# One state block per corner of the array, and triangular output products cut into 64x64 tiles, in a fused RWKV and feed-forward kernel

## The chip, the cores and the metric

The kernel runs on one NeuronCore of a Trainium2 chip. The metric is the device time of one execution in microseconds (us). Times below are the median of three runs, and one further execution was profiled. TensorE is called PE in the profile (PEld is its loading of weights), VectorE DVE, ScalarE ACT, GpSimd POOL, SyncE SP.

## The reference

A linear attention with a decaying state runs over 768 steps for 4 batches of 8 heads of width 48, and its output goes through a feed-forward layer with 384 inputs and 2048 hidden columns. Cut to what matters:

```
for t in range(S):
    y[:, :, t] = r_t @ (state + (u * k_t) v_t^T)
    state = w_t[:, None] * state + k_t v_t^T
x = y.transpose(0, 2, 1, 3).reshape(B * S, H * D)      # 3072 x 384
h = x @ w_in
out = (h * sigmoid(1.702 * h)) @ w_out
```

## The kernel before

**Chunks.** Tokens go in 24 chunks of 128 (t = 0 to 23), six per batch, so that chunks 0, 6, 12 and 18 start without a state and chunks 5, 11, 17 and 23 leave none. Heads go in four pairs p; the even head of a pair lies on partitions 0 to 63 (16 of them zeros) and the odd one on 64 to 111. `chunk(t)` is a generator of twelve steps: two scans of the decays (L252, L258), the scaled k and r in `kq` (L273, L274), the diagonal `s`, the decay of the old state (L292), the transposes of k (ps_t), `update` (products ps_u at L332 and the new state), `diagonal` (eight ACT copies into `am`, L321), the scores (L359) copied into `am` under the mask `after` (L362), the output products, and `split` (L222 on ACT, L223 on DVE), which leaves the output as a high and a low part in the tile x. `fill_x` (L425, POOL) moves parts of x for the feed-forward layer when a group of four chunks is complete.

**Two layouts.** For chunks 0 to 11 the state `sf` of a pair is a block of 112 rows by 96 columns, in which the rows of one head meet zeros in the columns of the other. The output goes to one tile, ps_y: L399 multiplies `am` (128 tokens by 128 tokens, zero below the diagonal) by v, with the two heads in two column halves of the array (128x64 tiles), and L407 adds the state's part, also with 128x64 tiles. For chunks from 12 on (`cross`) the state is `sx`, 48 columns per pair without zeros, two of the four pairs have their heads swapped, and the output goes to two tiles ps_c: L371 does the state's part in 64x64 tiles (four at once), L377 the part of `am` in 128x64 tiles over all 128 columns.

**Feed-forward.** 96 tasks (six groups i of four chunks, 16 slices f of hidden columns each). A task multiplies x by a slice of w_in into a tile ph (two buffers), `gelu` makes gh, gf (ACT) and gl (DVE), and two tasks later the second product adds into three tiles po. Tasks 32 to 94 run as `rows_of`: their products are cut into two row halves of the array (64x128 tiles) that run beside each other. When the last second product of a group is done, `store` copies its three po tiles to ob on ACT (L587), and the next group's second products write the same three tiles.

**Order.** Everything is in the order written: first the string RAMP (tasks before 32 and the chunks 0 to 12, part of 13), then `rest`, which gives each chunk's steps a place relative to the tasks. An output and its `split` stand right before the `update` and `diagonal` of the next chunk. Each engine works through its own queue in that order. At two places, after chunk 16 and after chunk 20, a group ends there: ACT's queue has the split, the eight `diagonal` copies, then the three ob copies, then the next gelu.

Of the kernel before, what the change touches and what calls it, by code (L numbers as in the profile page):

```python
# [21 lines left out]
P = 128  # L22
NP = H // 2
R = 2 * D
HB = 64
# [59 lines left out]
def rwkv_ffn_kernel(ctx: ExitStack, tc, wkr, vp, vrk, ub, w_in, w_out, masks, vt, uc, out):  # L85
# [26 lines left out]
    after = cp.tile([P, C], F32, name="after")  # L112
# [5 lines left out]
    after_b = after.bitcast(I32).unsqueeze(1).broadcast_to([P, NP, C])  # L118
    u_heads = hm[:, 2:].rearrange("r (p h) -> r p h", h=2)
# [10 lines left out]
    states = [at.tile([R2, TOP + NP * R], F32, tag=f"sf{i}", name="sf") for i in range(2)]  # L130
    crossed = [at.tile([R2, TOP + NP * D], F32, tag=f"sx{i}", name="sx") for i in range(2)]
# [7 lines left out]
    def behind_moves(dma):  # L139

        if len(moves) == 2 * NM:
            tc.add_manual_dep(dma.ins, moves[-1], SYNC, reason="the first group's x is wanted sooner")
        return dma

    def load(t):
# [7 lines left out]
        if t < CROSS:  # L153
            for c0, c1 in ((0, n), (n, a.shape[1])) if t < 2 else ((0, a.shape[1]),):
                if c0:
                    yield
                behind_moves(queue[0].dma_start(a[first:last, c0:c1], rows[:, c0:c1]))
        else:
            for c0, w in ((1, CW), (n, C), (n + NP * C, C)):
                for odd in range(2):  # L160
                    cols = slice(c0 + odd * 2 * w, c0 + (odd + 1) * 2 * w)
                    for half in range(2):
                        dst, src = TOP + half * D, (half ^ odd) * D
                        queue[0].dma_start(a[dst : dst + D, cols], wkr[t, src : src + D, cols])  # L164
        yield
        assert t < 3 or t - 3 in weighed
        queue[0].dma_start(v[:, TOP:], vrk[t, :, 0:DM])
        if t >= WHOLE:
            rk = pools["late"].tile([P, 2 * DM], F32, tag="rk", name="rk_t")
            queue[0].dma_start(rk, vrk[t, :, DM:])  # L170
# [68 lines left out]
    def chunk(t):  # L239
# [7 lines left out]
        first, final = t % CB == 0, (t + 1) % CB == 0  # L247

# [24 lines left out]
        V.tensor_tensor(kf, k, li[:, :, 1:CW], op=ALU.mult)  # L273
# [37 lines left out]
        cross = t >= CROSS  # L311
        name = lambda p, r_: 2 * p + (r_ ^ p // 2 if cross else r_)

        def diagonal():

            for h in range(2):
                x_ = at.tile([P, NP, C], F32, tag=f"am{h}", name="am")
                am.append(x_)
                for p in range(NP):
                    j = name(p, h)  # L320
                    A.activation(x_[:, p], ident, AF.Copy, scale=s[:, j : j + 1])  # L321

        def update():
# [9 lines left out]
            if cross:  # L333
                new = state[t] = crossed[t % 2]
                flat = ps_u.rearrange("r p d -> r (p d)")
                if sf is None:
                    A.copy(new[:, TOP:], flat)
                else:
                    V.tensor_tensor(new[:, TOP:], flat, sf[:, TOP:], op=ALU.add)
                return  # L340
            new = state[t] = states[t % 2]
            news, olds = (y[:, TOP:].rearrange("r (p h d) -> r p h d", p=NP, h=2) for y in (new, states[1 - t % 2]))
            for h in range(2):
                if sf is None:
                    A.copy(news[head(h), :, h], ps_u[head(h)])
                else:
                    V.tensor_tensor(news[head(h), :, h], ps_u[head(h)], olds[head(h), :, h], op=ALU.add)
# [13 lines left out]
        for h in range(2):  # L361
            V.copy_predicated(am[h], after_b, ps[h])  # L362
        yield
        cs = slice(col * C, (col + 1) * C)
        if cross:
            ps = [ps_a.tile([R2, 2, C], F32, tag="psa", name=f"ps_c{r_}") for r_ in range(2)]
            each = [(p, r_, r_ ^ p // 2) for p in (0, 2, 1, 3) for r_ in range(2)]
            if sf is not None:
                for p, r_, o in each:
                    c = p * D  # L370
                    T.matmul(  # L371
                        ps[r_][head(o), p % 2], sf[head(r_), c + o * TOP : c + HB], qf[head(r_), p],
                        start=p in (0, 2), stop=False, skip_group_check=True,
                    )
            for p, r_, o in each:
                c = (2 * p + o) * D
                T.matmul(  # L377
                    ps[r_][head(o), p % 2], v[:, c + o * TOP : c + HB], am[r_][:, p],
                    start=sf is None and p in (0, 2), stop=p in (1, 3), skip_group_check=True,
                )  # L380
# [39 lines left out]
    def fill_x(x, c0, c1, cross=False):  # L420

        for m in range(NM):
            for i, dst in enumerate((R2, 0)):
                j = TOP * (2 * m + i + 1)
                move = G.dma_start(  # L425
                    x[dst : dst + TOP, :, m ^ 2 * (cross and i == 0), c0:c1].bitcast(F32),
                    x[j : j + TOP, :, NM ^ 2 * (cross and j >= HB), c0:c1].bitcast(F32),
# [17 lines left out]
    def first_product(j, task):  # L445
# [5 lines left out]
        x = xs.get((i, 0), xs[i])  # L451
# [69 lines left out]
    def first_rows(j, half):  # L521
# [5 lines left out]
        for n in range(3 * NM):  # L527
# [5 lines left out]
                half, ("h", j), parts[j], w, xs[i][:, x, c ^ 2 * (half and starts[i] >= CROSS), cs],  # L533
# [47 lines left out]
    def store(i, start, N, order=range(NM)):  # L581
# [12 lines left out]
        xs.pop((i, 0), None)  # L594
# [5 lines left out]
    with tc.manual_schedule():  # L600
# [17 lines left out]
        def do(token):  # L618
# [7 lines left out]
            elif kind == "x":  # L626
                group, col = where[i]
                if col == CHUNKS[group] - 1:
                    fill_x(xs[group], 0, (col + 1) * C, i >= CROSS)
            elif kind == "c":  # L630
                x = xs[i, 0] = new_x(i)
                for c in range(NM):
                    for rows, src in ((slice(0, HB), c), (slice(HB, P), c ^ 2)):
# [188 lines left out]
```

## Time and profile before

| what | value |
|---|---|
| median of three runs | 507.99 us (507.67 to 508.84) |
| the profiled execution | 508.05 us |
| its span, first to last instruction | 506.1 us |
| PE, busy | 494.2 us, 98% |
| DVE, busy | 290.6 us, 57% |
| ACT, busy | 283.9 us, 56% |
| granted TensorE clock, mean | 0.997 of full speed |

The span and the profiled execution's time differ by 1.95 us, which lie before the first and behind the last instruction. Busy time is the union of an engine's instructions. The duration of one matmul contains its way through the array, so that matmuls overlap; how fast they follow one another is read from the distance of their starts.

### The profile page before, as it was taken

The numbers are of one execution on the slowest core, as the hardware profiler recorded it, in microseconds if no ns is written. First come the engines' busy times: TensorE is split into PE (matmuls) and PEld (weight loads), VectorE is DVE, ScalarE is ACT, GpSimd is POOL, SyncE is SP. The second block draws the span as 40 slices with busy tenths as digits, with TensorE's granted clock in tenths as the row PEclk, the third lists the DMA queues.
The fourth block names the chain that finished last, engine by engine and source line by source line (L and its number), as shares of the span: only waits on it lengthen the run. The fifth ranks groups of instructions, "written<-read, shape, count | busy, mean of one in ns | idle before, by whom it ended". The sixth has DMA issues, their size and how long they took to land.

```text
span 506.1 us, 11444 instructions
## 1 busy us (share of the span) xinstructions
PE 494.2 (98%) x4535; PEld 416.5 (82%) x4535; DVE 290.6 (57%) x451; ACT 283.9 (56%) x618; POOL 95.5 (19%) x200
## 2 busy tenths in 40 slices
PE   7999999999999999999999999999999999999994
PEld 3766777888888888888888888888888888888873
DVE  7899999999987213656456555555555322111210
ACT  4987889978865533465455465554564533323222
POOL 2002000000100200076304376303460002210000
PEclk9999999999999999999999999999999999999998
DMA  8996960125465300045112245111350001140001
GB/s 269 308 378 188 332 218 7 58 93 189 127 181 126 84 1 1 0 132 138 32 49 48 79 115 153 42 40 33 96 156 2 1 1 33 69 121 1 1 1 69
DMA packets 19471, 50.30 MB, mean 99 GB/s; under 512 B 4545, under 2 KB 8321, under 8 KB 19409
## 3 DMA queue, kind: packets, MB, share of 16 engines
q1 hardware_dynamic: 11664, 31.24, 19.3%
q0 software_dynamic: 7344, 17.72, 13.7%
q8 instruction: 38, 0.62, 0.5%
q10 hardware_dynamic: 400, 0.53, 0.3%
q14 instruction: 25, 0.20, 0.1%
HBM read 40.82 MB, written 4.72 MB: 90 GB/s over the span
## 4 chain that ended last, share of the span: by engine, by line
PE 82%; DVE 5%; ACT 4%; DMA 2%; issue 1%; POOL 1%; SPq 0%; ACTq 0%; DVEq 0%
PE po L512 26%; PE ph L512 24%; PE ps_s L359 3%; PE po L486 3%; PE ph L454 3%; PE po L487 3%; PE po L488 3%; PE ph L455 3%; PE ph L456 3%; PE ps_c L377 2%; DMA raw<-in_w_in 2%; PE ps_y L399 1%; PE ps_u L332 1%; PE ps_c L371 1%; PE ps_y L407 1%
## 5 line engine op out<-in xcount | busy, mean ns | idle before, releaser
L512 PE MATMUL ph<-x,pair 64*128 64x512 f32 x1134 | 185.5, 376 | 0.0
L472 DVE TENSOR_TENSOR gl<-gf,gh 128x512 fp32r<-128x512 f32 x96 | 66.3, 690 | 183.5 <-ACT gf L471 182.7
L512 PE MATMUL po<-gh,pair 64*128 64x512 f32 x768 | 157.6, 384 | 0.2 <-SPq L517 0.2
L512 PEld LDWEIGHTS ph<-x,pair 64*128 64x128 f32 x1134 | 143.5, 186 | 14.1
L471 ACT ACTIVATE gh<-ph 128x512 fp32r<-128x512 f32 x84 | 50.1, 597 | 157.7 <-PE ph L512 137.0
L512 PEld LDWEIGHTS po<-gh,pair 64*128 64x128 f32 x768 | 95.7, 186 | 10.4 <-issue 1.1
L512 PE MATMUL po<-gl,pair 64*128 64x512 f32 x384 | 99.2, 376 | 0.0
L425 POOL DMA_DIRECT2D x<-x x36 | 18.2, 512 | 248.5 <-DVE x L223 207.4
L321 ACT ACTIVATE am<-ident,s 128x128 f32<-128x128 f32 x192 | 58.8, 396 | 2.5 <-issue 1.5
L164 POOL DMA_DIRECT2D wkr_t<-in_wkr x108 | 53.8, 505 | 10.9 <-DVE kq L273 6.2
L512 PEld LDWEIGHTS po<-gl,pair 64*128 64x128 f32 x384 | 50.0, 186 | 4.8
L471 ACT ACTIVATE gf<-ph 128x512 f32<-128x512 f32 x84 | 49.8, 593 | 0.0
L454 PE MATMUL ph<-x,pair 128*128 128x512 f32 x99 | 39.0, 394 | 0.4 <-ACT gf L467 0.4
L456 PE MATMUL ph<-x,pair 128*128 128x512 f32 x99 | 38.0, 384 | 0.2 <-DVE pair L213 0.2
L455 PE MATMUL ph<-x,pair 128*128 128x512 f32 x99 | 37.9, 383 | 0.0
L486 PE MATMUL po<-gh,pair 128*128 128x512 f32 x96 | 37.8, 394 | 0.0
L488 PE MATMUL po<-gl,pair 128*128 128x512 f32 x96 | 36.9, 385 | 0.0
L487 PE MATMUL po<-gh,pair 128*128 128x512 f32 x96 | 36.8, 383 | 0.0
L228 ACT ACTIVATE junk<-lp 112x1032 bf16<-112x1032 f32 x24 | 25.6, 1068 | 12.3 <-DVE lp L258 12.2
L252 DVE TENSOR_TENSOR_SCAN lp<-wkr_t,d1r 112x516 f32<-112x516 f32 x24 | 29.4, 1225 | 1.3 <-DMA wkr_t<-in_wkr 1.0
L258 DVE TENSOR_TENSOR_SCAN lp<-wkr_t,d1f 112x516 f32<-112x516 f32 x24 | 29.4, 1225 | 0.1
L362 DVE COPY_PREDICATED am<-after,ps_s 128x512 f32<-128x512 int32 x40 | 26.9, 727 | 1.4 <-PE ps_s L359 1.2
(92 smaller groups left out, 645.0 us busy)
## 6 DMA issues: line engine op xcount, KB each, us to landing
wkr_t<-in_wkr SPq DMA_DIRECT2D x10, 770.5 KB, 5.3
raw<-in_w_out SPq DMA_DIRECT2D x6, 1024.0 KB, 11.4
raw<-in_w_in SPq DMA_DIRECT2D x5, 1024.0 KB, 10.9
wkr_t<-in_wkr POOLq DMA_DIRECT2D x72, 48.0 KB, 2.1
rk_t<-in_vrk POOLq DMA_DIRECT2D x9, 384.0 KB, 3.5
out_t<-ob POOLq DMA_DIRECT2D x12, 256.0 KB, 2.7
v_t<-in_vrk SPq DMA_DIRECT2D x15, 192.0 KB, 4.6
rk_t<-in_vrk SPq DMA_DIRECT2D x7, 384.0 KB, 3.4
```

The costliest lines, as they stand in the source:

```text
L164: queue[0].dma_start(a[dst : dst + D, cols], wkr[t, src : src + D, cols])
L252: V.tensor_tensor_scan(li.rearrange("r p c -> r (p c)")[:, ::-1], w1[:, ::-1], d1r.rearrange("r p c -> r (p c)")[:, ::-1], 0.0, op0=ALU.mu ...
L321: A.activation(x_[:, p], ident, AF.Copy, scale=s[:, j : j + 1])
L454: T.matmul(o, h_, halves(x[:, 0, c, cs], plain), start=c == 0, stop=False)
L455: T.matmul(o, h_, halves(x[:, 1, c, cs], plain), start=False, stop=False)
L456: T.matmul(o, l_, halves(x[:, 0, c, cs], plain), start=False, stop=c == NM - 1)
L471: A.activation(g, ph, AF.Gelu_apprx_sigmoid, scale=1.0 / W_SCALE)
L472: V.tensor_tensor(gl, gf, gh.bitcast(F32), op=ALU.subtract)
L486: T.matmul(o, h_, halves(gh, plain), start=first, stop=False, skip_group_check=True)
L487: T.matmul(o, l_, halves(gh, plain), start=False, stop=False, skip_group_check=True)
L488: T.matmul(o, h_, halves(gl, plain), start=False, stop=f == NF - 1, skip_group_check=True)
L512: mm = T.matmul(by_twos(out), w[rows], halves(x[rows]), start=start, stop=stop, skip_group_check=True)
```

## The change

Chunks 0 to 11 take the state without zero blocks too: `sf` has 48 columns per pair, the decay handles 192 columns instead of 384, the new state is one operation instead of two, and the state's product for the even head uses rows and columns 0 to 63, for the odd head rows and columns 64 to 111 (two opposite corners of the array, both into ps_y).

For chunks from 12 on, the products of `am` and v are cut in two halves of 64 source tokens. The half-matrix of `am` that is zero for the earlier 64 target tokens is left out: per pair and head there is one 64x64 tile over 128 columns and one over 64. The two halves go to two tiles ps_c, which hold partial sums; a tile `yt` collects them (two ACT copies, four DVE additions), and then `split` works on all of yt. In the two swapped pairs the order of source tokens is turned by halves, so that both row halves of the array get the same work: the loads of v, r, k bring swapped halves, `kf` is written turned, and a turned identity and a turned mask are made once in the step `u`. The layout of x is the same for all groups, so the step `c` (six POOL moves) goes.

```
-    states = [at.tile([R2, TOP + NP * R], ...) for i in range(2)]
-    crossed = [at.tile([R2, TOP + NP * D], ...) for i in range(2)]
+    states = [at.tile([R2, TOP + NP * D], ...) for i in range(2)]
...
+        if cross:
+            pairs_ = slice(0, NP // 2)
+            V.tensor_tensor(kf[:, pairs_], k[:, pairs_], li[:, pairs_, 1:CW], op=ALU.mult)
+            V.tensor_tensor(out_[:, :, ::-1], *ins_, op=ALU.mult)
+        else:
+            V.tensor_tensor(kf, k, li[:, :, 1:CW], op=ALU.mult)
...
-            for h in range(2):
-                if sf is None:
-                    A.copy(news[head(h), :, h], ps_u[head(h)])
-                else:
-                    V.tensor_tensor(news[head(h), :, h], ps_u[head(h)], olds[head(h), :, h], op=ALU.add)
+            if sf is None:
+                A.copy(new[:, TOP:], flat)
+            else:
+                V.tensor_tensor(new[:, TOP:], flat, sf[:, TOP:], op=ALU.add)
...
         if cross:
-            ps = [ps_a.tile([R2, 2, C], F32, tag="psa", name=f"ps_c{r_}") for r_ in range(2)]
+            ps = [ps_a.tile([R2, NP, C], F32, tag="psa", name=f"ps_c{r_}") for r_ in range(2)]
...
-            for p, r_, o in each:
-                c = (2 * p + o) * D
-                T.matmul(
-                    ps[r_][head(o), p % 2], v[:, c + o * TOP : c + HB], am[r_][:, p], ...
+            for p, halves_ in ((0, (0, 1)), (2, (1, 0)), (1, (0, 1)), (3, (1, 0))):
+                for i_ in halves_:
+                    for r_ in range(2):
+                        o = r_ ^ p // 2
+                        c, rows, c0 = (2 * p + o) * D, slice(i_ * HB, (i_ + 1) * HB), HB * (i_ ^ p // 2)
+                        T.matmul(
+                            ps[i_][head(o), p, c0:], v[rows, c + o * TOP : c + HB], am[r_][rows, p, c0:], ...
...
-            for b, y in enumerate(ps):
-                split(*(xs[i][0:R2, n_, 2 * b : 2 * b + 2, cs] for n_ in range(2)), y)
+            yt = at.tile([R2, NP, C], F32, tag="rku", name="yt")
+            for b, y in enumerate(ps):
+                two = slice(2 * b, 2 * b + 2)
+                A.copy(yt[:, two], y[:, two])
+            for b, y in enumerate(ps):
+                two = slice(2 - 2 * b, 4 - 2 * b)
+                for rows, cols in ((slice(0, HB), slice(HB, C)), (slice(HB, R2), slice(HB if sf is None else 0, C))):
+                    V.tensor_tensor(yt[rows, two, cols], yt[rows, two, cols], y[rows, two, cols], op=ALU.add)
+            split(*(xs[i][0:R2, n_, :, cs] for n_ in range(2)), yt)
...
-                    c = 2 * p * D + h * HB
+                    c = p * D
                     T.matmul(
-                        ps[head(h), p], sf[:, c : c + HB - h * TOP], qf[:, p],
+                        ps[head(h), p], sf[head(h), c + h * TOP : c + HB], qf[head(h), p],
...
             elif kind == "u":
                 nc.sync.dma_start(u_sb, ub)
-                for x in crossed:
+                for x in turned, masked[:, 1]:
                     G.memset(x, 0.0)
+                for h in range(2):
+                    rows, cols = (slice(i * HB, (i + 1) * HB) for i in (h, 1 - h))
+                    A.copy(turned[rows, cols], ident[rows, rows])
+                A.copy(masked[HB:, 1, 0:HB], after[HB:, HB:])
+                A.copy(masked[0:HB, 1, HB:], after[0:HB, 0:HB])
+                V.memset(masked[HB:, 1, HB:], 1.0)
...
-                    if post and j == len(TASKS) - WHOLE:
-                        yield f"c{len(CHUNKS) - 1}"
```

On PE, the output of chunk 13 (line, operation, tile written <- tiles read, shape of what is written) stands as follows before, ahead of the next chunk's ps_u:

```order
L371 MATMUL ps_c_2566<-kq,sx 48x128
L371 MATMUL ps_c_2567<-kq,sx 64x128
L377 MATMUL ps_c_2566<-am,v_t 64x128
L377 MATMUL ps_c_2567<-am,v_t 48x128
L377 MATMUL ps_c_2566<-am,v_t 48x128
L377 MATMUL ps_c_2567<-am,v_t 64x128
...
L332 MATMUL ps_u<-v_t,kt 64x48
```

and now, where the first half of what follows the state's products is:

```order
L388 MATMUL ps_c_2568<-kq,sf 48x128
L388 MATMUL ps_c_2569<-kq,sf 64x128
L397 MATMUL ps_c_2568<-am,v_t 64x128
L397 MATMUL ps_c_2568<-am,v_t 48x128
L397 MATMUL ps_c_2569<-am,v_t 64x64
L397 MATMUL ps_c_2569<-am,v_t 48x64
L397 MATMUL ps_c_2569<-am,v_t 48x128
L397 MATMUL ps_c_2569<-am,v_t 64x128
L397 MATMUL ps_c_2568<-am,v_t 48x64
L397 MATMUL ps_c_2568<-am,v_t 64x64
...
L355 MATMUL ps_u<-v_t,kt 64x48
```

Eight products became sixteen, half of them over 64 columns; what stands around them is the same.

On ACT, behind the output of chunk 16, where a group of tasks ends (x is the split's result, am the diagonal, ob the copies of po, gh the next gelu), before:

```order
L222 CAST x<-ps_c_3453 112x2x128
L222 CAST x<-ps_c_3454 112x2x128
L321 ACTIVATE am<-ident,s 128x128 x8
L587 ACTIVATE ob<-po_2362 128x512
L587 ACTIVATE ob<-po_2388 128x512
L587 ACTIVATE ob<-po_2390 128x512
L471 ACTIVATE gh<-ph 128x512
```

and now:

```order
L408 COPY yt<-ps_c_3491 112x256
L408 COPY yt<-ps_c_3492 112x256
L237 CAST x<-yt 112x4x128
L344 ACTIVATE am<-ident,s 128x128 x2
L344 ACTIVATE am<-turned,s 128x128 x2
...
L614 ACTIVATE ob<-po_2363 128x512
L614 ACTIVATE ob<-po_2389 128x512
L614 ACTIVATE ob<-po_2391 128x512
L498 ACTIVATE gh<-ph 128x512
```

One cast more stands ahead of the diagonal, and it reads yt, which DVE finishes. On DVE at the same place, before:

```order
L472 TENSOR_TENSOR gl<-gf,gh 128x512
L223 TENSOR_TENSOR x<-ps_c_3453,x 112x2x128
L223 TENSOR_TENSOR x<-ps_c_3454,x 112x2x128
L258 SCALAR_TENSOR_TENSOR lp<-wkr_t,d1f 112x516
L268 TENSOR_TENSOR rk_t<-rk_t 128x384
```

and now:

```order
L499 TENSOR_TENSOR gl<-gf,gh 128x512
L412 TENSOR_TENSOR yt<-yt,ps_c_3491 64x2x64
L412 TENSOR_TENSOR yt<-yt,ps_c_3491 48x256
L412 TENSOR_TENSOR yt<-yt,ps_c_3492 64x2x64
L412 TENSOR_TENSOR yt<-yt,ps_c_3492 48x256
L238 TENSOR_TENSOR x<-yt,x 112x4x128
L274 SCALAR_TENSOR_TENSOR lp<-wkr_t,d1f 112x516
```

Four additions stand between the ACT copies of yt and the ACT cast that reads it; the subtraction of the split comes once, on all columns.

## Rows read from the trace of the kernel before

**Rows 1.** The page: busy time of the engines; shares of the chain that ended last.

```profile
PE 494.2 (98%) x4535; PEld 416.5 (82%) x4535; DVE 290.6 (57%) x451; ACT 283.9 (56%) x618; POOL 95.5 (19%) x200
...
PE 82%; DVE 5%; ACT 4%; DMA 2%; issue 1%; POOL 1%; SPq 0%; ACTq 0%; DVEq 0%
```

**Rows 2.** Windows: length, busy us of PE, PEld, DVE, ACT, POOL, granted clock, DMA.

```profile
0.00:46.00 46.00, 41.73 (x394) 27.32 (x394) 41.03 (x65) 32.90 (x72) 6.66 (x26) 1.00 0.92 295
...
86.00:205.00 119.00, 118.82 (x866) 101.64 (x865) 84.39 (x128) 76.26 (x165) 5.97 (x12) 1.00 0.32 92
205.00:440.00 235.00, 235.00 (x2556) 205.22 (x2556) 116.62 (x201) 120.33 (x286) 78.58 (x155) 1.00 0.24 62
```

**Rows 3.** Timeline of PE at chunk 19's output: start, length, line, tiles, count.

```profile
344.13 0.67 PE L371 MATMUL ps_c<-kq,sx 64*64 64x128 f32 x16
344.73 1.09 PE L377 MATMUL ps_c<-am,v_t 128*64 128x128 f32 x16
345.65 0.62 PE L332 MATMUL ps_u<-v_t,kt 128*48 128x48 f32 x16
```

**Rows 4.** The chain in order of time, chunk 7's output: start, us, what.

```profile
123.07 0.88 PE ps_y L407 x16
123.94 0.45 PE ps_u L332 x15
```

**Rows 5.** Groups by shape: busy us, mean ns of one, idle time before.

```profile
L292 DVE TENSOR_TENSOR sf<-sf,lp 112x384 f32<-112x384 f32 x10 | 5.5, 549 | 0.0
L292 DVE TENSOR_TENSOR sx<-sx,lp 112x192 f32<-112x192 f32 x10 | 3.5, 348 | 0.0
L347 DVE TENSOR_TENSOR sf<-ps_u,sf 48x192 f32<-48x192 f32 x8 | 2.9, 361 | 0.1
L339 DVE TENSOR_TENSOR sx<-ps_u,sx 112x192 f32<-112x192 f32 x8 | 2.8, 349 | 0.0
L223 DVE TENSOR_TENSOR x<-ps_c,x 112x256 fp32r<-112x256 f32 x24 | 9.1, 420 | 10.1 <-ACT x L222 10.1
L222 ACT CAST x<-ps_y 112x512 fp32r<-112x512 f32 x12 | 6.9, 575 | 6.3 <-PE ps_y L407 6.2 <-PE ps_y L399 0.2
```

**Rows 6.** The chain in order of time, 47 to 58 us.

```profile
47.79 8.93 DMA raw<-in_w_in
...
56.74 1.18 ACT raw L202
```

**Rows 7.** Waits from 14 to 46 us: who for whom, total us, times, longest.

```profile
PEld ps_y L399 <- DVE am L362: 2.7, 6, 0.5
```

**Rows 8.** Timeline of PEld at 85 us, with idle time before and its releaser.

```profile
85.59 0.19 PEld L454 LDWEIGHTS ph<-x,pair 128*128 128x128 f32 x1 [0.80 <-ACT gf L467]
```

**Rows 9.** Timeline of ACT and PE behind chunk 18's output.

```profile
330.75 0.60 ACT L471 ACTIVATE gh<-ph 128x512 fp32r<-128x512 f32 x1 [0.92 <-PE ph L512]
331.24 0.59 ACT L471 ACTIVATE gf<-ph 128x512 f32<-128x512 f32 x1
...
334.03 1.67 PE L512 MATMUL ph<-x,pair 64*128 64x512 f32 x13
```

**Rows 10.** Timeline of ACT behind chunk 16's output, where a group ends.

```profile
289.53 0.65 ACT L222 CAST x<-ps_c 112x256 fp32r<-112x256 f32 x2 [1.17 <-PE ps_c L377]
290.06 2.45 ACT L321 ACTIVATE am<-ident,s 128x128 f32<-128x128 f32 x8
292.41 1.55 ACT L587 ACTIVATE ob<-po 128x512 f32<-128x512 f32 x3
```

**Rows 11.** Timeline of PEld at the same place.

```profile
293.04 0.18 PEld L512 LDWEIGHTS po<-gh,pair 64*128 64x128 f32 x1 [0.30 <-ACT ob L587]
```

**Rows 12.** Timeline of ACT behind chunk 20's output, where a group ends.

```profile
367.73 1.55 ACT L587 ACTIVATE ob<-po 128x512 f32<-128x512 f32 x3
```

**Rows 13.** Timeline of PEld at that place.

```profile
368.37 0.18 PEld L512 LDWEIGHTS po<-gh,pair 64*128 64x128 f32 x1
```

More of the change, by code (lines that the diff above doesn't have):

```diff
@@ L143, in behind_moves, with bring @@
         return dma
+    def bring(dst, src, turn):
+        if not turn:
+            queue[0].dma_start(dst, src)
+            return
+        dst, src = (y.rearrange("s (n q) -> s n q", q=DM) for y in (dst, src))
+        queue[0].dma_start(dst[:, :, 0 : DM // 2], src[:, :, 0 : DM // 2])
+        for h in range(2):
+            rows, others = (slice(g * HB, (g + 1) * HB) for g in (h, 1 - h))
+            queue[0].dma_start(dst[rows, :, DM // 2 :], src[others, :, DM // 2 :])
     def load(t):
@@ L158, in load @@
         else:
[L159 to L164, printed above, removed]
+            w_, kr = slice(1, n), slice(n, a.shape[1])
+            for cols, n_ in ((w_, 1), (kr, 2)):
+                dst, src = (y[:, cols].rearrange("r (n q) -> r n q", n=n_) for y in (a, wkr[t]))
+                one, two = (slice(h * dst.shape[2] // 2, (h + 1) * dst.shape[2] // 2) for h in range(2))
+                queue[0].dma_start(dst[TOP:R2, :, one], src[:, :, one])
+                for h in range(2):
+                    rows = slice(TOP + h * D, TOP + (h + 1) * D)
+                    queue[0].dma_start(dst[rows, :, two], src[(1 - h) * D : (2 - h) * D, :, two])
         yield
         assert t < 3 or t - 3 in weighed
-        queue[0].dma_start(v[:, TOP:], vrk[t, :, 0:DM])
+        bring(v[:, TOP:], vrk[t, :, 0:DM], t >= CROSS)
         if t >= WHOLE:
             rk = pools["late"].tile([P, 2 * DM], F32, tag="rk", name="rk_t")
-            queue[0].dma_start(rk, vrk[t, :, DM:])
+            bring(rk, vrk[t, :, DM:], t >= CROSS)
             loaded[t].append(rk)
@@ L361, in chunk @@
         for h in range(2):
-            V.copy_predicated(am[h], after_b, ps[h])
+            if cross:
+                V.copy_predicated(*(y.rearrange("s (a b) c -> s a b c", a=2) if y is not after_x else y for y in (am[h], after_x, ps[h])))
+            else:
+                V.copy_predicated(am[h], after_b, ps[h])
         yield
@@ L532, in first_rows @@
             on_rows(
-                half, ("h", j), parts[j], w, xs[i][:, x, c ^ 2 * (half and starts[i] >= CROSS), cs],
+                half, ("h", j), parts[j], w, xs[i][:, x, c, cs],
                 half == 0 and n == 0, half == 1 and end, half == 0 and end,
@@ L628, in do @@
                 if col == CHUNKS[group] - 1:
[L629 to L633, printed above, removed]
-                        G.dma_start(x[rows, :, c].bitcast(F32), xs[i][rows, :, src].bitcast(F32))
+                    fill_x(xs[group], 0, (col + 1) * C)
             elif kind == "u":
                 nc.sync.dma_start(u_sb, ub)
-                for x in crossed:
+                for x in turned, masked[:, 1]:
                     G.memset(x, 0.0)
+                for h in range(2):
+                    rows, cols = (slice(i * HB, (i + 1) * HB) for i in (h, 1 - h))
[3 more added lines that the diff above has]
+                V.memset(masked[HB:, 1, HB:], 1.0)
             elif kind == "M":
```

55 lines of the change are left out of this document (25 added, 30 removed).

## The prediction

> **What bounds the kernel now.** I read the page first, for the busy shares and the chain that ended last: PE is busy 98% of the span, and PE holds 82% of the chain [rows 1]. A share is an average, so windows by stage come next [rows 2]. From 205 to 440 us PE is busy for all of 235.00 us, while DVE and ACT work about half of it; from 86 to 205 us it is busy 118.82 of 119. In these stretches only what PE itself does counts, or something late enough to make PE wait. In the first 46 us it is otherwise: PE and DVE are both nearly full (41.73 and 41.03), so DVE may count there. The granted clock is 1.00 in all three, so no term below has a part for it. The timeline of PE around an output gives the pace of the products [rows 3, 4], and the timelines of ACT and PEld around the ends of groups show who is late for whom [rows 9 to 13].
>
> **Pace of the products.** On PE the distance of starts counts. Before chunk 19's `update`, the 16 products of `am` and v start at 344.73 and the next kind at 345.65: 0.92 us [rows 3]. Chunk 7's 16 state products run in 0.88 to 0.45 us of chain without a gap: 123.94 − 123.07 = 0.87 [rows 4]. Two of these run at once (two column halves), so 8 rounds take 0.87, a round of 128 columns 0.109. L371's 64x64 products go four at once: 16 in 4 rounds, 0.44, but L377 starts 0.60 behind them (344.13 to 344.73). The 0.16 left is the price of a change of tile size: the next shape starts only when the last is through. I take 0.14 a change, because the first weight load of a new run is partly hidden.
>
> **Before 86 us: −1.0 (bounds −1.7 to 0).** A decay of 192 columns takes 348 ns where 384 took 549, so −0.20; a state addition is one of 349 where two of 361 stood, so some −0.35 to −0.37 [rows 5]. Three chunks (1 to 3) do this in the DVE chain that leads to the first x: 3 × 0.55 = −1.65. In that stretch PE has other products in its queue and waits for DVE only six times, 2.7 us in all [rows 7], so I credit about half, −0.8. Behind it a transfer of 8.93 us and ACT's work on what it brings decide [rows 6], both of which shift along. Near 86 us PE waits 0.80 us for a gelu of ACT [rows 8], so shorter DVE and ACT work of chunk 4 still counts there: −0.2. If the transfer starts by its own queue, nothing is left; if all of the DVE time counts, −1.7.
>
> **Outputs of chunks 5 and 7 to 11: +1.5 (0 to +2.6).** The state product goes from 128x64 to two opposite 64x64 corners. Two tiles still run at once, 8 rounds of 128 columns: no gain in pace. But L399 before it stays 128x64 and L332 behind it is 128x64, so where the sequence ran without a gap [rows 4] there are now two changes. Five chunks (5, 7, 8, 9, 11) get two; chunk 10, where scores of another tile size follow already, gets one. 11 × 0.14 = 1.5. The upper end takes 0.24 a change, half again the 0.16 of the row, 11 × 0.24 = 2.6; the lower lets corner tiles start beside the old shape. Decay and addition become shorter on DVE here too, but PE does not wait for them [rows 2].
>
> **Products of `am` and v in chunks 12 to 23: −2.5 (−2.5 to 0).** Of each quarter of the array, four halves of 128 columns remain and four of 64: 4 × 0.109 + 4 × d. Eight L332 products of 48 columns in two column halves take 0.45 [rows 4], so d is about 0.057, not much above half of 0.109. Each tile then takes 0.66 where it took 0.87: −0.21 a chunk, × 12 = −2.5. If the short ones take as long as the long ones (their weights are as many), the term is 0.
>
> **Changes of tile size in these chunks: −0.3 (−0.5 to 0).** The state's products and those of `am` now have one tile size, which removes a change; behind them L332 of the next chunk has another, which adds one. In seven chunks that cancels. Chunks 16, 22 and 23 have no L332 right behind: −0.14 each. Chunk 18 has no state's products but L332 behind it: +0.14. Chunk 12 gains nothing.
>
> **The split: +3.9 (0 to +5).** Before, `split` was two ACT casts and two DVE subtractions out of PSUM, and the subtraction of DVE held nobody. Now ACT copies twice, DVE adds four times, then one ACT cast of all 512 columns, which must wait for DVE. ACT's queue is in order, so behind this cast stand `diagonal` (8 copies, 2.45 us), and at two places the ob copies too. From the first split cast to the diagonal took 290.06 − 289.53 = 0.53 us [rows 10]. Now: the two copies 0.65 (as L222's pair did); the four additions, of which the last two must wait for the second copy. No row shows an addition of 64x128 or 48x256; the nearest are 112x192 at 349 ns, 48x192 at 361 and 112x256 at 420 [rows 5]. I take 0.28 for the small and 0.42 for the large, 1.4 in all, partly beside the second copy: 1.3. The cast of 112x512 takes 575 ns [rows 5] as one instruction, about 0.5 in pace. With what passes between the engines I have some 2.55 instead of 0.53: ACT is 2.0 us later (1.4, if the additions run at half that price beside the copies, to 2.5, if DVE is busy when the copies end).
>
> Who waits for it? Of twelve outputs, ten stand where the next thing that PE wants of ACT is a gelu or the diagonal itself for a later place. Behind chunk 18, ACT's gelu itself waited 0.92 us for PE, and it ends (331.24 + 0.59 = 331.83) 2.2 us ahead of PE's next run of ph at 334.03 [rows 9]: together 3.1 us of slack, more than 2.0. These cost nothing; if slack fell under 2.0 at all ten, each tenth of a microsecond would cost 1.0.
>
> At the ends of groups, behind chunks 16 and 20, it is otherwise. The first ob copy starts at 292.41 [rows 10], and PE's first second product of the next group, which writes the same po, is released at 293.04, having waited 0.30 us for that copy already [rows 11]. At the other place the copy starts at 367.73 [rows 12] and the product loads at 368.37 [rows 13], the same 0.64 us later: no slack. So ACT's 2.0 us pass to PE undiminished, and as PE is full, they are never made good: 2 × 2.0 = 4.0, less 0.1 since PE reaches these places a little later itself. If the wait is covered by other PE work, it is 0; at 2.5 a place, 5.
>
> **Hidden or small.** `kf` in two pieces costs DVE some 0.15 us a chunk, under a DVE that works 116.62 of 235.00 us [rows 2]. Four small ACT copies and a memset in the step `u` come once, 0 to +0.3, taken as 0. Loads are twelve instead of fourteen a chunk, and the six POOL moves of the step `c` go; with DMA at 0.24 of its time there [rows 2] I take 0 (−0.2 to +0.2).
>
> **Sum.** −1.0 + 1.5 − 2.5 − 0.3 + 3.9 = +1.6 on the profiled execution's 508.05 us, 0.06 above the median: 509.6.
>
> **The rivals.** Measurement tells about 0.2% from no change here, that is 1.0 us: faster means under 507.0, slower over 509.0.
>
> Stall not passed on (faster). If the additions are cheap or PE has other work queued until the ob copy is there, the last term falls to 0 to 0.5: 508.05 − 2.3 + 0 = 505.7. For it: DVE is half idle there [rows 2]. Against it: both rows show PE's load right behind the copy. It decides from where ACT's delay is under the slack, which these rows give as zero.
>
> Short products at the price of long ones (the change does not do what it says). The half with 64 columns loads as many weights, and the pace may be set by the load: the 2.5 is lost, 512.1. Against it: L332's 0.057 with 64 or 48 weight columns; for it: PEld is busy 205 of 235 us [rows 2].
>
> Two row halves, one tile. In chunks 0 to 11 both corners write ps_y, a single tile; L371's row halves had one tile each. If the corners take turns, 8 rounds become 16: +0.87 × 6 outputs = +5.2, 514.8. No row shows two row halves on one tile, and nothing in the trace says that they run beside each other. The Trainium skill, "TensorEngine Tiling (Array Packing)", among its restrictions, says that different row tiles cannot access one PSUM bank at the same time; by that rule the corners would take turns at best, as in this rival.
>
> Stall about half, or the early gain whole: 507.2 to 508.9, about no change.
>
> **How the numbers follow.** The forecast, a stall of 1.4 to 2.5 us at both places with the other terms near my values, 508.4 to 510.8: 0.50. No stall: 0.18. Half a stall or a larger early gain: 0.12. Short products dear: 0.14. Corners in turns: 0.06. Faster takes nearly all of the second, 0.16; same takes the half stall, the rest of the second and the low edge of the forecast, 0.12 + 0.02 + 0.08 = 0.22; slower the rest, 0.62. The range leaves out the corners in turns, the lower part of no stall and the upper part of dear products: 506.4 to 512.0.
>
> **What would show it.** PE's load for po behind chunks 16 and 20 waiting some 2 us for ob, and on ACT the cast of yt waiting for DVE ahead of the diagonal (split). The starts of the `am` products to L355 some 0.7 us apart, with 64-column ones at about 0.06 (products). Gaps of 0.1 to 0.2 on both sides of the corner products in chunks 5 to 11 (changes). PE's stretch without gaps beginning some 1 us earlier than 86 (early). It would be wrong if chunk 23's split, the last before the tail, or the x of a group became late as a whole, which these rows do not price.

## The result and the profile after

The changed kernel took 512.36 us (median of 20 runs, 510.82 to 514.75) beside 507.87 for the kernel before: a ratio of 1.0086 (95% interval 1.0076 to 1.0096), so 0.9% slower. The forecast was 509.6 us with a range up to 512.0. The sign is right and the size is not: +4.4 us by that ratio where +1.6 was forecast. The profiled execution took 512.72 us with a span of 510.8, which is 4.7 longer than the 506.1 before.

The page of the changed kernel, its busy times and its row of the granted clock in 40 slices (of 12.8 us each):

```profile
PE 495.6 (97%) x4727; PEld 416.4 (82%) x4727; DVE 302.8 (59%) x492; ACT 290.4 (57%) x632; POOL 89.7 (18%) x176
...
PEclk9999999999999999999999989999999999999998
```

PE's work is 1.4 us longer than in [rows 1], but the span is 4.7 longer: PE now stands still for some time, and in one slice near 295 us its clock is not full. The windows that answer to [rows 2], and then two narrow ones around 295 us (columns as there):

```profile
86.00:205.00 119.00, 118.20 (x857) 99.63 (x856) 79.74 (x122) 74.68 (x165) 5.97 (x12) 1.00 0.32 92
205.00:440.00 235.00, 230.86 (x2708) 202.09 (x2709) 133.84 (x249) 124.78 (x293) 75.79 (x135) 0.99 0.23 62
...
292.00:295.00 3.00, 0.85 (x7) 0.43 (x7) 2.22 (x3) 3.00 (x10) 0.00 (x0) 0.96 0.00 0
295.00:298.00 3.00, 3.00 (x24) 2.82 (x26) 0.93 (x2) 2.71 (x6) 2.97 (x6) 0.50 0.55 208
```

From 292 to 295 PE works 0.85 of 3 us; in the next three it is busy all the time, but at a granted clock of 0.50, that is 1.2 instead of 2.4 GHz.

Where the time goes is read by taking the same feed-forward product (the n-th one on PE) in both timelines and comparing its start. "After, again" is another profiled execution of the same changed kernel (e11 below).

| n-th product, what lies before it | before | after | difference | after, again |
|---|---|---|---|---|
| 1, the first | 47.21 | 45.81 | −1.40 | 45.65 |
| 145, near 86 us | 85.59 | 84.14 | −1.45 | 84.72 |
| 409, outputs of chunks 5 to 11 | 172.25 | 172.90 | +0.65 | 173.16 |
| 1201, chunks 12 to 16 | 291.47 | 290.97 | −0.50 | 291.23 |
| 1225, end of a group | 295.12 | 298.50 | +3.38 | 297.13 |
| 1777, chunks 17 to 20 | 367.25 | 369.97 | +2.72 | 368.60 |
| 1801, end of a group | 370.73 | 375.27 | +4.54 | 373.90 |
| 2209, chunks 21 to 23 | 423.06 | 426.92 | +3.86 | 425.55 |
| 2233, behind chunk 23 | 425.65 | 430.22 | +4.57 | 428.85 |
| end | 506.10 | 510.76 | +4.66 | 510.23 |

Four places lose: the outputs of chunks 5 to 11 (+2.1), the two group ends (+3.9 and +1.8), and the stretch behind chunk 23 (+0.7). The outputs of chunks 12 to 23 win, 1.15 + 0.66 + 0.68 = 2.5.

**The group ends.** The timeline of ACT behind chunk 16, then DVE's additions there, then the rows of PEld and PE; ACT and PEld answer to [rows 10] and [rows 11]:

```profile
289.06 0.65 ACT L408 COPY yt<-ps_c 112x256 f32<-112x256 f32 x2 [0.86 <-PE ps_c L397]
291.29 0.62 ACT L237 CAST x<-yt 112x512 fp32r<-112x512 f32 x1 [1.58 <-issue]
291.81 0.69 ACT L344 ACTIVATE am<-ident,s 128x128 f32<-128x128 f32 x2
...
294.16 1.53 ACT L614 ACTIVATE ob<-po 128x512 f32<-128x512 f32 x3
```

```profile
289.74 1.47 DVE L412 TENSOR_TENSOR yt<-yt,ps_c 64x128 f32<-64x128 f32 x4 [0.82 <-ACT yt L408]
...
294.79 0.28 PEld L539 LDWEIGHTS po<-gh,pair 64*128 64x128 f32 x1 [2.55 <-ACT ob L614]
...
294.79 0.79 PE L539 MATMUL po<-gh,pair 64*128 64x512 f32 x1 [2.15 <-ACT ob L614]
```

From the first copy to the diagonal there are now 291.81 − 289.06 = 2.75 us, where [rows 10] have 0.53. Of these 1.58 are ACT standing in front of its cast. Its releaser is printed as "issue"; in the groups by shape the same cast has DVE's yt as its releaser for 14.0 of 18.4 us, and here DVE's four additions end at 289.74 + 1.47 = 291.21, right ahead of it. The groups by shape (busy us, mean ns of one, idle time before):

```profile
L412 DVE TENSOR_TENSOR yt<-yt,ps_c 48x256 f32<-48x256 f32 x20 | 8.5, 424 | 0.3
L412 DVE TENSOR_TENSOR yt<-yt,ps_c 64x128 f32<-64x128 f32 x24 | 6.7, 279 | 10.3 <-ACT yt L408 9.9
L237 ACT CAST x<-yt 112x512 fp32r<-112x512 f32 x12 | 7.4, 618 | 18.4 <-DVE yt L412 14.0 <-issue 4.4
```

The additions take 424 and 279 ns, as estimated (0.42 and 0.28). PE's load for po waited 0.30 in [rows 11] and 2.55 here; PE itself stands still for 2.15. The waits of PEld over the whole span, one row for both ends of groups, and PE at the second of them, which answers to [rows 13] (there: no wait):

```profile
PEld po L539 <- ACT ob L614: 4.5, 2, 2.5
...
373.19 0.48 PE L539 MATMUL po<-gh,pair 64*128 64x512 f32 x1 [1.55 <-ACT ob L614]
```

**The outputs.** PE's timeline at chunk 7 before the change, the same after it, and after it at chunk 20, whose products answer to [rows 3]. Each of these products stands in the trace as two matmuls:

```profile
121.98 1.09 PE L399 MATMUL ps_y<-am,v_t 128*64 128x128 f32 x16
122.90 1.05 PE L407 MATMUL ps_y<-kq,sf 112*48 112x128 f32 x16
123.77 0.62 PE L332 MATMUL ps_u<-v_t,kt 128*48 128x48 f32 x16
...
121.02 1.09 PE L426 MATMUL ps_y<-am,v_t 128*64 128x128 f32 x16
122.04 1.08 PE L434 MATMUL ps_y<-kq,sf 64*64 64x128 f32 x16
123.05 0.67 PE L355 MATMUL ps_u<-v_t,kt 128*64 128x48 f32 x16
...
366.06 0.67 PE L388 MATMUL ps_c<-kq,sf 64*64 64x128 f32 x16
366.54 0.86 PE L397 MATMUL ps_c<-am,v_t 64*48 64x64 f32 x32
367.33 0.67 PE L355 MATMUL ps_u<-v_t,kt 128*64 128x48 f32 x16
```

In chunk 7 it takes 123.05 − 121.02 = 2.03 us from the first `am` product to L355, where before it took 123.77 − 121.98 = 0.92 + 0.87 = 1.79: two changes of tile size cost 0.24. The corner products themselves need 1.01 with a change in it, so they keep the old pace. In chunk 20 the 32 products of `am` take 0.79 with a change behind them, where 16 took 0.92. The state's products, which now have no change behind them, take 0.48 where they took 0.60 [rows 3], 0.12 again for one change.

**Behind chunk 23.** DVE's timeline, then PEld:

```profile
425.37 1.45 DVE L412 TENSOR_TENSOR yt<-yt,ps_c 64x128 f32<-64x128 f32 x4 [0.81 <-ACT yt L408]
427.55 0.69 DVE L238 TENSOR_TENSOR x<-yt,x 112x512 fp32r<-112x512 f32 x1 [0.74 <-ACT x L237]
428.28 0.15 DVE L739 CAST acc<-ps_n 1x1 int32<-1x1 f32 x1
```

```profile
429.46 0.30 PEld L539 LDWEIGHTS po<-gh,pair 64*128 64x128 f32 x4 [0.85 <-SPq L544]
```

SP's own wait for that cast, from 400 to 440 us (total, times, longest), before and after:

```profile
SPq L717 <- DVE acc L714: 0.3, 1, 0.3
...
SPq L742 <- DVE acc L739: 1.3, 1, 1.3
```

The kernel counts checks of its inputs in `acc`, and SP loads that count (L742). DVE casts it at 428.28, behind the additions and the subtraction; SP, whose queue is in order too, waits for it, and the signals that SP passes between the row halves of PE's products (L544) stand behind it. So PE's load waits 0.85 us for SP, where before no such wait was over 0.3.

### The profile page after: what moved, and what is told of

Same layout as the page of the kernel before. It is cut to its first block, busy times and chain, and to the rows that moved or that the text cites. A ratio compares the mean times of both kernels' runs of the same rounds, so it can differ in the third digit from the quotient of the medians.

```text
span 510.8 us, 11883 instructions
## 1 busy us (share of the span) xinstructions
PE 495.6 (97%) x4727; PEld 416.4 (82%) x4727; DVE 302.8 (59%) x492; ACT 290.4 (57%) x632; POOL 89.7 (18%) x176
## 5 line engine op out<-in xcount | busy, mean ns | idle before, releaser
L539 PE MATMUL po<-gh,pair 64*128 64x512 f32 x768 | 159.3, 386 | 4.4 <-ACT ob L614 3.7
L539 PEld LDWEIGHTS po<-gh,pair 64*128 64x128 f32 x768 | 97.3, 187 | 15.0 <-ACT ob L614 4.5
L539 PE MATMUL po<-gl,pair 64*128 64x512 f32 x384 | 100.7, 377 | 0.0
L539 PEld LDWEIGHTS po<-gl,pair 64*128 64x128 f32 x384 | 51.4, 187 | 4.9
L344 ACT ACTIVATE am<-ident,s 128x128 f32<-128x128 f32 x144 | 45.8, 391 | 2.6 <-issue 1.5
L243 ACT ACTIVATE junk<-kq 112x1024 bf16<-112x1024 f32 x24 | 25.3, 1056 | 1.6 <-DVE kq L298 1.5
L528 PE MATMUL idle<-d1r 112*128 112x512 bf16 x78 | 21.6, 419 | 2.8 <-POOL v_t L669 2.8
```

What stands on the lines that cost most here:

```text
L243: A.activation(junk[:, 0 : x.shape[1]], x, AF.Square, accum_out=acc[0:R2, i : i + 1])
L344: A.activation(x_[:, p], turned if cross and p // 2 else ident, AF.Copy, scale=s[:, j : j + 1])
L539: mm = T.matmul(by_twos(out), w[rows], halves(x[rows]), start=start, stop=stop, skip_group_check=True)
```

## The experiments

Each was timed beside runs of the kernel before on the same chip, and the ratio is to those. Four chips were used, on which the kernel before took 507.7 to 508.2 us, so a difference of under half a microsecond between times of different experiments says little. "The changed kernel" is the base of the diffs unless another is named. The expectations stand as they were written before each run.

### e1: the cast on DVE

```
-            split(*(xs[i][0:R2, n_, :, cs] for n_ in range(2)), yt)
+            hi, lo = (xs[i][0:R2, n_, :, cs] for n_ in range(2))
+            V.tensor_copy(hi, yt)
+            V.tensor_tensor(lo, yt, hi.bitcast(F32), op=ALU.subtract)
```

> In chunks 12 to 23 the high part of x is cast on DVE, so ACT only copies twice and its queue holds no instruction that waits for DVE ahead of the diagonal. Theory (two stalls behind chunks 16 and 20, made by ACT's cast that waits for the additions, 2.2 and 1.8 us, and a lower TensorE clock behind them in about half of the runs): both waits for ob fall to about 0.3 us, the granted clock is 0.997, the time is 512.4 - 4.0 - 1.2 = about 507.2 us, less than 0.2% from the kernel before. Rival (the 4.5 us were lost in the array, by changes of tile size and corners): within 1 us of 512.4. Rival (the wait only moves to DVE, whose gl then comes late): 509 to 511, and PE waits for gl.

Measured: 507.31 us, ratio 0.9983 (0.9969 to 0.9996). ACT's timeline and PEld's row at the same place:

```profile
289.75 0.65 ACT L408 COPY yt<-ps_c 112x256 f32<-112x256 f32 x2 [0.86 <-PE ps_c L397]
290.28 0.70 ACT L344 ACTIVATE am<-ident,s 128x128 f32<-128x128 f32 x2
...
292.63 1.54 ACT L616 ACTIVATE ob<-po 128x512 f32<-128x512 f32 x3
```

```profile
293.26 0.18 PEld L541 LDWEIGHTS po<-gh,pair 64*128 64x128 f32 x1 [0.34 <-ACT ob L616]
```

From copies to diagonal there are 0.53 us again and PE waits 0.34, as before the change; the clock is full there. The stalls and what follows them are worth 512.4 − 507.3 = 5 us: both rivals (array, DVE) forecast at least 509.

### e12: the same work, the cast behind the diagonal

```
+            parts_ = [xs[i][0:R2, n_, :, cs] for n_ in range(2)]
+            if t in (16, 20):
+                later.append(lambda: split(*parts_, yt))
...
             part()
+            if part is diagonal and later:
+                later.pop()()
```

> The changed kernel, with the cast still on ACT, but behind chunks 16 and 20 it stands after the eight diagonal copies, so that ACT has them to do while DVE adds; the work of every engine is the same. Theory (ACT's place in line, not its amount of work, makes the stall: 1.58 us of each wait is ACT waiting for DVE): the ob copies come 1.58 us sooner, PE's waits for them fall from 2.5 and 1.9 us to some 0.9 and 0.3, the clock stays at 0.996 or more, and the time is 512.4 - 3.2 - 0.9 = 508.3 us. Rival (the longer ACT work itself or the changes in the array make it slow): 511.5 to 512.4.

Measured: 508.06 us, ratio 0.9998 (0.9986 to 1.0011).

```profile
291.05 0.65 ACT L412 COPY yt<-ps_c 112x256 f32<-112x256 f32 x2 [0.86 <-PE ps_c L401]
291.58 0.70 ACT L346 ACTIVATE am<-ident,s 128x128 f32<-128x128 f32 x2
...
293.93 0.60 ACT L237 CAST x<-yt 112x512 fp32r<-112x512 f32 x1
294.44 1.55 ACT L622 ACTIVATE ob<-po 128x512 f32<-128x512 f32 x3
```

```profile
295.08 0.18 PEld L547 LDWEIGHTS po<-gh,pair 64*128 64x128 f32 x1 [0.86 <-ACT ob L622]
```

ACT never stands between 291.05 and 295.9, and the ob copies come 3.4 us behind the first yt copy instead of 5.1. No engine does less; a place in line alone is worth 512.4 − 508.1 = 4.3 us, 3.4 of them at the two group ends and the rest fits the clock, which stays at 0.995 or more in all twelve runs. With e1 this settles the stall. A wait of 0.86 us is left at the first end, as forecast.

### e4: the stall filled with products of zeros; e11: the changed kernel again

Of e4 (zeros are added to a finished ph tile, ten times, at the two group ends):

```
+            if opens and k == early_end:
+                for _ in range(FILL):
+                    T.matmul(parts[j - 1], zeros[:, 0:P], zeros[:, 0:WIDE], start=False, stop=False, ...)
```

> As the changed kernel, but at the two places where PE waits for ob, ten products of zeros are added to a finished ph tile, so that PE has about 2.1 us of work in the wait; nothing that PE waits for comes sooner. Theory (PE's clock falls because PE stands idle there): the granted clock is 0.996 to 0.997 in every run, the runs lie within 1 us of each other, and the median is that of the undisturbed half of the runs, about 511.2 us. Rival (the lower clock comes by chance or from other causes than the idle time): median about 512.4 us with runs up to 514.7, as before.

> The changed kernel itself, unaltered, beside the others. Theory (the lower clock behind the first stall comes in about half of the executions and costs 1.65 us): 512.4 us median, runs with a mean clock of 0.996 or more near 511.2, runs below near 513.5.

Measured: e4 511.74 us (511.49 to 511.97), ratio 1.0074 (1.0060 to 1.0088); e11 512.43 us (511.73 to 515.74), ratio 1.0097. PE's timeline and the window of e4, then the window of e11, whose profiled execution happens to have kept its clock:

```profile
292.01 2.33 PE L604 MATMUL ph<-d1r 112*128 112x512 bf16 x10
...
290.00:296.00 6.00, 6.00 (x53) 4.11 (x51) 3.10 (x6) 5.06 (x14) 1.32 (x3) 1.00 0.03 12
```

```profile
296.00:300.00 4.00, 4.00 (x47) 3.60 (x46) 3.01 (x6) 1.97 (x4) 3.15 (x6) 1.00 0.75 249
```

PE does useless work for as long as it would have stood still, and in all six runs of e4 the mean clock is 0.995 to 0.998. Their median is 0.5 above the forecast: the zeros (2.33 us) are longer than the second standstill (1.55), and the two group ends take 0.7 us more than in e11. The runs spread over 0.5 us instead of 3.9, but a spread alone is no sign of the clock: e1, with no stall and clocks of 0.995 to 0.998, spreads over 3.1 us. The nine of the 20 runs of the changed kernel whose mean clock is 0.996 or 0.997 lie at 510.82 to 511.95; the other eleven (0.989 to 0.995) at 512.32 to 514.75. The stretch from the 409th to the 2209th product takes 254.02 us in the execution that lost its clock and 252.39 in the one that kept it: the price of the lower clock is 1.63 us. e11's profiled execution has a mean clock of 0.995 with nothing lost at the group ends; its lower clock lies in the last 5 us of the span. So a mean of 0.995 doesn't tell whether a run lost its clock, e11's six runs (0.992 to 0.996) don't decide on "about half", and the slowest of them (515.74) is not explained by this.

### e2: all products of am over 128 columns

```
-                        ... c0 = ..., HB * (i_ ^ p // 2)
+                        ... c0 = ..., 0
```

> The products of am and v in chunks 12 to 23 stay in 64x64 tiles, but all run over 128 columns (the zero quarters are multiplied too). Theory (64 columns cost about half): each output 0.21 us longer, 512.4 + 2.5 = 514.9 us. Rival (weight loads set the pace, the short ones save nothing): 512.4 us, no difference.

Measured: 514.80 us (511.62 to 516.98), ratio 1.0124. PE at chunk 20:

```profile
369.46 1.06 PE L397 MATMUL ps_c<-am,v_t 64*48 64x128 f32 x32
370.45 0.67 PE L355 MATMUL ps_u<-v_t,kt 128*64 128x48 f32 x16
```

0.99 us instead of 0.79: the short products are worth 0.20 an output, 2.4 in all, as forecast. The six runs spread over 5.4 us, so it is the trace that gives the price: between the same feed-forward products the stretches with the outputs of chunks 12 to 23 take 2.4 us more in all than in the changed kernel.

### e3 and e5: zero blocks in chunks 0 to 11, without and with the cast on DVE

Both give chunks 0 to 11 the state of the kernel before (block states, two additions, 128x64 products of all rows); e5 has e1's edit as well.

```
-                        ps[head(h), p], sf[head(h), c + h * TOP : c + HB], qf[head(h), p],
+                        ps[head(h), p], sf[:, c : c + HB - h * TOP], qf[:, p],
```

> Chunks 0 to 11 keep the state with zero blocks of the kernel before; only the part of the change for chunks from 12 on is made. Theory (from the traces: 1.45 us won before 86 us; behind it five outputs lose 0.28, one 0.12, and two transposes wait 0.6 in all, 2.1 together): 512.4 - 0.6 = 511.8 us. Rival (two row halves on one tile take turns, 0.87 for each of six outputs): 507 to 508. Rival (the shorter DVE work early is worth its full 1.65 and nothing is given back): 514.

> As the run with the cast on DVE (507.31 us), and chunks 0 to 11 keep the state with zero blocks of the kernel before. No stall and no lower clock blurs the comparison, so it prices the change of chunks 0 to 11 alone. Theory (behind 86 us that change costs 2.0 us in every trace so far; ahead of 86 us it wins about 1, since the start of the first feed-forward product differs by up to 2 us between executions of any kernel): 507.3 - 1.0 = 506.3 us. Rival (the 1.45 us of the one profiled execution are the true early gain): 506.8. Rival (nothing is won early, 2.0 lost): 505.3.

Measured: e3 512.46 us (ratio 1.0087), 0.1 above the changed kernel where −0.6 was expected: the varying clock behind the stall (0.992 to 0.997 in its six runs) hides what was asked. Its profiled execution lost the clock at the same place as the changed kernel's; the window of e3:

```profile
290.00:300.00 10.00, 7.85 (x65) 6.77 (x63) 5.63 (x9) 6.25 (x17) 3.85 (x7) 0.83 0.36 118
```

e5 took 506.48 us, ratio 0.9966 (0.9951 to 0.9981), −0.8 from e1: between the theory's 506.3 and the first rival's 506.8, which these runs can't tell apart. The traces agree behind 86 us: from the 145th to the 409th product the kernels with blocks take 86.6 us (before, e3, e5), those with corners 88.4 to 88.8 (both profiles of the changed kernel, e1, e2) or 88.1 (e7 below). Taking turns (+5.2) does not happen.

### e6 and e9: the state's products ahead of those of am

Both with e1's edit; e6 in all chunks up to 11, e9 in chunks 5 to 11 alone and with e7's edit.

```
+        if sf is not None:
+            for p in range(NP):
+                for h in range(2):
+                    T.matmul(ps[head(h), p], sf[head(h), ...], qf[head(h), p], start=p == 0, stop=False, ...)
         for p in range(NP):
             for h in range(2):
                 T.matmul(ps[head(h), p], v[:, ...], am[h][:, p], start=sf is None and p == 0, ...)
```

> As the run with the cast on DVE (507.31 us), but in chunks 1 to 11 the corner products of the state stand ahead of the products of am. Their tile size then has a neighbour of another size on one side where a change stood anyway, and five of the six outputs behind 86 us have one change less. Theory (0.12 to 0.14 us for each change of tile size): 0.6 to 0.7 us less, 506.6 us, and the state's products also cover waits for the mask. Rival (it is the corners themselves that are slow, on one tile, and order doesn't matter): 507.3 us and the same 2.03 us from the first product to L355.

> As the run with the cast on DVE and the count ahead of the last split (506.18 us), and in chunks 5 to 11 alone the corner products of the state stand ahead of those of am. Theory (two changes of tile size in each output cost 0.24 us, one less saves about 0.1, and L355 behind products of its own tile size another 0.05; the earlier run with this order in all chunks lost its gain to a lower clock at 40 to 50 us, which chunks 1 to 4 in their old order avoid): 0.15 for each of five outputs, and up to 0.6 of waits of the transposes, so 504.8 to 505.4 us, clock 0.996 or more. Rival (the order has no worth, and the lower clock of that run had other causes): 506.2 us or lower clocks again.

Measured: e6 507.64 us (ratio 1.0000), e9 506.64 us (ratio 0.9969). Both miss. PE of e6 at chunk 7, then its windows at 40 to 48 us:

```profile
121.95 1.08 PE L429 MATMUL ps_y<-kq,sf 64*64 64x128 f32 x16
122.96 1.09 PE L436 MATMUL ps_y<-am,v_t 128*64 128x128 f32 x16
123.88 0.62 PE L355 MATMUL ps_u<-v_t,kt 128*48 128x48 f32 x16
...
40.00:44.00 4.00, 2.82 (x19) 1.69 (x17) 4.00 (x7) 2.76 (x4) 2.64 (x5) 1.00 0.35 65
44.00:48.00 4.00, 4.00 (x40) 3.10 (x39) 3.76 (x7) 3.95 (x9) 0.88 (x4) 0.67 0.43 95
```

The price of a change is confirmed (1.93 from the first product to L355, 0.10 less). But in e6 PE comes to stand 1.2 us in 40 to 44 us, and the clock falls to 0.67 behind that; that the one makes the other is not tried here. e9 keeps its clock and still gains nothing: each output behind 86 us then costs 0.14 instead of 0.28, but PE waits 0.3 to 0.4 us each time near 105 and 131 us. At 131 us it is PE's transposes:

```profile
130.95 0.57 PE L331 MATMUL ps_t<-ident,kq 112*128 112x112 f32 x4 [0.39 <-DVE kq L297]
```

### e7, e8 and e10: the count ahead of the last split

All with the cast on DVE; e8 has zero blocks in chunks 0 to 11, e10 in chunks 6 to 11 alone.

```
+            if token == f"a{NT - 1}" and told[token] == 12:
+                tally()
```

> As the run with the cast on DVE (507.31 us), but the count that decides on the slow path is made ahead of the last split: DVE's cast of it stands before the four additions instead of behind the split. Theory (behind chunk 23 PE waits 0.85 us for SP's signals between the row halves, because SP waits for that cast, which the additions made late): the wait goes, 0.5 to 0.7 us less, 506.7 us. Rival (SP's wait is hidden or the wait has another cause): 507.3 us.

> Cast on DVE, zero blocks in chunks 0 to 11, and the count ahead of the last split. If the terms add up: 507.3 - 1.0 - 0.6 = 505.7 us, 0.5% faster than the kernel before, which is the 2.5 us of the products of am in chunks 12 to 23 with none of the waits. Rival (the terms overlap or a wait remains): 506.5 or more.

> As the run with the cast on DVE and the count ahead of the last split, but the corners are used in chunks 0 to 5 only, and zero blocks in chunks 6 to 11. Theory (corners win about 0.9 us ahead of the first feed-forward product and lose 0.28 a chunk behind it): with corners everywhere 506.18, with blocks everywhere 506.47, so about 505.0 us here. Rival (no early gain, only run-to-run differences of the start): 506.2 to 506.5, as both.

Measured: e7 506.18 us, ratio 0.9971 (0.9953 to 0.9989); e8 506.47, ratio 0.9971 (0.9954 to 0.9988); e10 504.34, ratio 0.9927 (0.9911 to 0.9942). DVE and PEld of e7 behind chunk 23:

```profile
418.84 0.14 DVE L546 CAST acc<-ps_n 1x1 int32<-1x1 f32 x1 [0.28 <-PE ps_n L545]
418.95 1.45 DVE L412 TENSOR_TENSOR yt<-yt,ps_c 64x128 f32<-64x128 f32 x4
...
418.62 0.09 PEld L545 LDWEIGHTS ps_n<-oks 128*1 128x1 f32 x2 [0.58 <-DVE oks L543]
...
420.10 0.30 PEld L553 LDWEIGHTS po<-gh,pair 64*128 64x128 f32 x4 [0.20 <-SPq L558]
```

The count is cast ahead of the additions and the wait for SP (0.85 us in the changed kernel, 0.7 in e1) is down to 0.20: from the 2209th to the 2233rd product 2.59 us, as before the change, where the changed kernel has 3.30 and e1 3.14. But the count's own product now waits for DVE, a load for 0.58 us, and the stretch from the 1801st to the 2209th product grows from 51.44 us in e1 to 51.80. So 0.2 of the 0.55 us are left, and that e7 lies 1.1 us under e1 (0.6 by the ratios, whose intervals overlap) is not shown to come from the count.

e8 came out 0.8 above its expectation, at its rival's 506.5 ("a wait remains"), and the wait for `oks` stands in its trace too. e10 came out 0.7 below: corners until chunk 5 and blocks from there beat either alone, by intervals that do not meet. e10 is the fastest version of all, 0.7% under the kernel before. Its profiled execution, though, is its slowest run, 508.83 us where the other six took 503.97 to 504.97; there PE waits in front of the first feed-forward product for the DMA that moves x. The wait of e10's loads (total, times, longest):

```profile
PEld ph L494 <- DMA x<-x: 1.8, 1, 1.8
```

## Why the prediction was wrong

Taken in the order of its sum, for the profiled execution where nothing else is said:

- **Before 86 us, −1.0.** −1.45 in the profiled execution. This is the least certain term: the first feed-forward product starts anywhere between 45.6 and 47.8 us in ten profiles of kernels with corners (mean 46.6), and between 46.6 and 48.0 in four with blocks (mean 47.3). The prediction left out the DMA that moves x. With corners PE is through with what stands ahead of that product at 45.2 to 46.3 us (47.8 in e6, behind its lower clock), some 1.5 us sooner than with blocks; but in six of the ten PE then waits 0.36 to 1.60 us for x, in none of the four with blocks. So some 1.5 us are won where x is there in time (in the timed runs e10 even lies 2.1 us under e8), an execution can give nearly all of it back, and what makes x late in some is open.
- **Outputs of chunks 5 to 11, +1.5.** +2.1. The step was right and the term a little small: two changes cost 0.24 (0.12 each; 0.14 taken), but L355 behind corners also runs 0.04 longer, 0.28 together. Most of the rest is PE's transposes waiting for DVE's kq, 0.8 in this execution. In e7's, where they wait 0.2, the stretch takes 88.12 us, 1.5 more than with blocks.
- **Products of `am`, −2.5, and changes, −0.3.** −2.5 together. e2 confirms 0.20 an output for the short products.
- **The split, +3.9.** The stall was right in place, cause and size: 5.90 − 3.65 = 2.25 us at the first group end in the execution that kept its clock, and 1.82 at the second, 4.1 in all. e1 takes it away, e12 3.4 us of it.
- **The clock, 0.** Here the prediction failed. It read a granted clock of 1.00 in the trace of before and concluded that "no term below has a part for it", but its own next terms made PE stand still for 2 us, which the trace of before does not show from 86 us on. Behind the first standstill (PE idle 2.15 us) the clock fell to 1.2 GHz in the profiled execution, for 1.63 us more; behind the second (1.55 us) it did not. e4 shows the cause: with PE kept busy the loss goes, though the stall stays. Over the 20 runs it is worth some 512.4 − 511.1 (the median of the nine at 0.996 or more) = 1.25 us; e4, less its 0.7 us of surplus zeros, gives the same 511.1.
- **Behind chunk 23, 0.** Also left out: it was named as what would make the forecast wrong, but not followed to a number. It is +0.7: DVE's additions delay a cast of one number, SP waits for it, and SP's signals to PE are late. e7 takes this wait away, though it puts another of some 0.4 in its place.

So for the median, with the early gain as forecast: 1.6 forecast, 0.7 for the count, 0.6 for the outputs, 0.3 for products that won less, 0.2 for the stall and 1.25 for the clock make 4.65; the measured difference is 3.9 to 4.9. Without the clock it would have been about 511.1 us, inside the range.

Of the rivals, "stall not passed on" and "short products dear" did not occur (e1, e2), nor did the corners take turns: L434's 16 products take 1.01 us with a change in them, where turns would need 1.75. The Trainium skill, "TensorEngine Tiling (Array Packing)", Restrictions and Gotchas, says that different row tiles cannot access the same PSUM bank at the same time; here two row halves write ps_y at the old pace, so for these two corners, which write different partitions of it, the trace does not agree. Why they may is not tried here.

The other page that bears on it is "TensorE: Matmul & The Clock Gate" of the Trainium skill, Part 1: it names 1.2 GHz as the engine's state when idle and 2.4 GHz when busy. The trace has these two levels, 1.00 and 0.50; but the half clock of the row at 295 us stands behind the idle time, while PE is busy for all of 3.00 us. That a standstill of 2.15 us can bring it about, and need not, is what the runs add.

## What to carry to other kernels

When a change puts an instruction that waits for another engine into a queue that is worked in order, price what stands behind it, most of all copies that free the accumulators of the busiest engine; moving the waiting instruction behind work that is ready (e12) adds no work and here brought the time back to that of the kernel before. A stall on a full TensorE has two prices, the standstill and the clock behind it, and the second comes in some executions only, so that it is looked for in the clock of each run. Follow delayed work of a side engine to its last reader, however small: here one number, cast 2 us later, held up SP and through it PE. And more than one execution is worth profiling: the profiled one of e10 lost 4.5 us against the others.

## What the runs showed of the hardware

- A standstill of PE of 2.15 us was followed by about 3 us at half clock in two profiled executions (the changed kernel, 0.50 from 295 to 298 us, and e3) and by none in two others (e11 and e2); standstills of 1.55 us at the second group end were followed by none in all four. Ten products of zeros in place of the first (e4) kept the clock at 1.00.
- Products in two opposite 64x64 corners of the array with one output tile run at the pace of two column halves: 1.01 us for 16 with 0.12 for a change in them, beside 0.87 without.
- A change of tile size between runs of products costs 0.12 us (0.24 for two, chunk 7), and one fewer saves 0.10 (e6).
- The cast of 112x512 from yt took 449 ns on DVE (e1) and 618 ns on ACT.
